# Seven q tiles in the ring of x tiles, and a new hand-over order, in a two-part long-convolution and state-space kernel

## Chip, cores and metric

One NeuronCore of a Trainium2 chip runs the whole program in one launch. The metric is the device time in microseconds; the median of eight runs of the kernel before is 384.14 us. PE is TensorE, ACT ScalarE, DVE VectorE, POOL GpSimd; SP is the engine that only issues DMAs here.

## The reference

Two branches share nothing and their results are put side by side, 1024 channels each, over 2048 time steps, in bf16.

```python
# A: a short convolution, a gate, a convolution as long as the sequence, a gate
k_shift = sum(k_pad[:, t:t + S, :] * shift_k[:, ks - 1 - t] for t in range(4))
kv = k_shift * v
y = irfft(rfft(pad(kv)) * rfft(pad(ssm_k)))[:, :S] + kv * ssm_D
a = q * y
# B: a diagonal complex recurrence between two complex matrices
Bu = einsum("bld,pd->blp", x, B_bar)
h_t = Lam_bar * h_(t-1) + Bu_t
b = 2 * einsum("blp,dp->bld", hseq, C).real + x * Dskip
out = concatenate([a, b], axis=-1)
```

## The kernel before

The program is a list of tasks. Each task is a small function that emits the instructions of one step for one tile; the string ORDER names them, and the last loop of `full_kernel` calls them one after the other. Each engine executes its own instructions in the order in which the tasks stand in ORDER, and semaphores tie the engines together. So ORDER is five queues written into one another. A task's name is followed by its indices: `y.15.1.3` is the last quarter of the second half of y for chunk 15.

**Branch B** works on 16 chunks of 128 time steps.
- `x.i` loads a chunk transposed into the ring `xT` of seven tiles (the first three by way of PE). `U.i.jp` (PE, L478, 32 matmuls) forms a quarter of B x in the PSUM pool `ps_u` (two banks); `ue.i.jp` (ACT, L480) evicts it into `u`.
- DVE runs the recurrence of a chunk: `r1.i` rotates u (L490), `r2.i` adds (L499), `ca.i` adds the carry (L504), `sc.i` scans (L510, two instructions), `cm.i` and `cy.i` make the next carry (L515, L517), `r3.i` rotates back (L490), `r4.i` adds (L523) and leaves h.
- `y.i.dh.part` (PE, L534 and L539) multiplies h by C and adds x D in `ps_y` (one bank), for the second half of the chunks 14 and 15 in `ps_u`. `ye.i.dh` (ACT, L549) evicts it, `yst.i` (POOL, L551) stores it, `ysh` (SP, L555) stores the last chunk in halves. `y.i.1.1` is the last reader of a tile of `xT`.

**Branch A** is a Fourier transform of length 4096 in two steps, with a trip to DRAM between them.
- `k`, `v` load; `kvm`, `kva`, `kvb`, `kvc` (DVE, L579 to L597) form kv; `am`/`ae`/`ast` do the first step for kv, `hT`/`hc`/`hm`/`he`/`hst` that for the filter.
- For 32 groups of frequencies: `lh`, `l`, `lw` load the group's data (tiles for two groups at a time), `sh` and `sk` (PE, L684) do the second step for filter and kv, `she` and `ske` (ACT) evict, `sw` (POOL) swaps halves by DMA, `pr` (DVE, L717) multiplies, `sa` (PE, L726) goes back, `sae` (ACT, L737) evicts, and `vst` (POOL, L739) stores two groups into the DRAM tensor `Vs`. The tile `vsb` that it stores from has two buffers.
- After the last `vst`, for 16 tiles: `vl.n` loads a tile of `Vs` (SP, L744, two DMAs, five buffers `vv`), `ql.n` loads q (SP, L749), `a3.n.w` (PE, L756) does the last step for one half, `a3e.n.w` (ACT, L764) evicts it into `ot`, `qm.n` multiplies by q (DVE, L775) and `ost.n` stores (POOL, L777). For the tiles 13, 14 and 15 `qp.n.w` (DVE, L770) multiplies straight from PSUM and `oth.n.w` (SP, L772) stores a half.

The q tiles have six buffers `qt` in a pool that opens where the pool of the `l2k` tiles (the kv spectra that `l` loads) ends, so no q tile loads before the last `sk`. The seventh waits until the `qm` of an earlier one has freed its buffer.

Of the kernel before, what the change touches and what calls it, by code (L numbers as in the profile page):

```python
# [24 lines left out]
def a_constants():  # L25
# [12 lines left out]
    for si in range(4):  # L38
# [23 lines left out]
CFG = dict(nx=3, hb=2, mt=2, u=4, xT=7, h=2, yo=2, ps_t=2, ps_u=2, ps_y=1, ps_a=3, kr=8, ld=5, acc=2, ysb=3,  # L62
           hk=3, hT=2, ysbh=2, l2=3, wts=4, swa=0, x16=3, hab=3, vsb=2, vv=5, qt=6, ot=6, bdve=8)
# [3 lines left out]
bl.0.1 bl.1.1 ld_w xl.0 k.-3 ld_par xl.1 ld_F bl.7.1 ld_G bl.0.0 k.-2 bT.0.1 bl.4.1 xl.2 bT.1.1 bc.0.1 k.-1 bl.2.1  # L67
wb.4 bc.1.1 bl.5.0 par_T wb.5 bl.4.0 p32 wb.6 bl.1.0 exp1 xt.0 bl.3.1 bl.2.0 xt.1 bl.3.0 wbe.4 dve2 k.0 x.0 bl.6.0
dve3 wb.7 x.1 x.3 wbe.5 bT.0.0 sm_pre exp2 wbe.6 hl.0.0 xt.2 wbe.7 bl.7.0 bc.0.0 tab.0 bl.5.1 wb.0 hl.0.1 wb.1 k.1 x.2
dd bT.7.1 wbe.0 bT.5.0 wbe.1 bl.6.1 tab.1 wb.2 wb.3 bc.5.0 v.0 bc.7.1 x.4 tab.2 bT.1.0 wbe.2 bT.2.1 wbe.3 bc.1.0 tab.3  # L70
k.2 x.5 bc.2.1 sin0 U.0.0 tab.4 hl.1.0 k.3 kvm.0 k.4 sin.2 bT.2.0 U.1.0 bc.2.0 ue.0.0 par_rest k.5 sin.4 bT.3.1 U.2.0
ue.1.0 kva.0 eo.0 bT.3.0 U.3.0 bc.3.1 bc.3.0 kvb.0 ue.2.0 stt.0 z1.1 bT.4.0 bT.4.1 kvm.1 ue.3.0 U.1.1 eo.1 U.3.1
ue.1.1 bc.4.1 k.6 bc.4.0 kva.1 z1.0 U.0.1 kvc.0 ue.3.1 kvb.1 eo.2 kvm.2 bT.6.0 bT.5.1 v.1 bc.6.0 am.0.0 U.2.1 ae.0.0
bc.5.1 ue.0.1 z1.2 kvm.3 bT.6.1 am.0.1 am.0.2 am.0.3 U.1.2 ae.0.2 ae.0.1 ue.2.1 stt.2 ast.0.0 ae.0.3 bT.7.0 ue.1.2
ast.0.1 bc.6.1 U.0.2 v.2 bc.7.0 stt.1 cl.0.1 cl.2.0 cl.1.0 U.0.3 kva.2 eo.3 kvc.1 ue.0.2 kvb.2 am.1.0 cl.2.1 ue.0.3
U.2.2 stt.3 kvc.2 z2 cT.2.0 r1.0 cl.3.1 cT.0.1 k.7 ae.1.0 U.3.2 cl.3.0 cc.2.0 cl.0.0 cx.5.0 ue.2.2 kva.3 cT.2.1 cc.0.1
U.2.3 cx.6.0 r2.0 ue.3.2 cc.2.1 hd.0 am.2.0 sc.0 k.8 hT.0.0 ue.2.3 cx.4.1 U.3.3 ae.2.0 hc.0.0 cx.7.1 am.2.1 am.1.1
ue.3.3 hT.0.1 ae.2.1 am.1.2 cx.7.0 cT.0.0 ae.1.1 ast.2.0 am.1.3 hc.0.1 U.1.3 ast.1.0 kvb.3 ae.1.2 cm.0 r3.0 ae.1.3
# [96 lines left out]
def full_kernel(ctx, tc, A_q, A_k, A_v, A_shift_k, A_ssm_k, A_ssm_D, B_x, B_Lre, B_Lim, B_Bre, B_Bim,  # L175
                B_Cre, B_Cim, B_log_dt, B_Dskip, out, cfg=None):
    c = dict(CFG)
    c.update(cfg or {})
    nc = tc.nc
    P = 128  # L180
    S, D = A_q.shape[-2], A_q.shape[-1]
# [73 lines left out]
    def atile(pool, tag, shape):  # L255
        return ap_pool(pool).tile(shape, BF16, name=tag, bufs=c[tag])
# [490 lines left out]
    def ql(n2):  # L747
        st["qt", n2] = atile("a3q", "qt", [P, D])
        spd(st["qt", n2][:], qr[:, n2, :])  # L749
# [90 lines left out]
```

## Time and profile before

| | us |
|---|---|
| median of eight runs | 384.14 (381.8 to 387.07) |
| the profiled execution, its own time | 382.61 |
| its span, from the first instruction to the last | 380.4 |
| PE busy | 361.1 |
| DVE busy | 329.7 |
| ACT busy | 276.8 |
| POOL busy | 124.8 |
| first load of `vv` is issued | 333.2 |
| last load of q is issued | 370.0 |

Busy shares are means over the span. The row of slices in the page shows where an engine is full; the windows give the same as microseconds for a stretch; the timeline gives the instructions one by one, with the idle time of the engine ahead of each in brackets and what ended it. A matmul is pipelined: in the timeline pairs of matmuls on 512 columns follow one another every 0.43 us, though one of them is shown with 379 ns.

### The profile page before, as it was taken

What the parts mean: (1) busy time and instruction counts of PE and PEld (TensorE: products, weight loads), DVE (VectorE), ACT (ScalarE), POOL (GpSimd) and SP (SyncE); (2) the same over time, 40 slices, a digit from 0 to 9 for tenths busy, and PEclk for the clock granted to TensorE, in tenths of its full rate; (3) what the DMA queues carried; (4) which work ended last, traced back from release to release, by engine and by line L of the source; (5) the groups of instructions that cost most, each with busy time, mean ns of one, the idle gap of its engine ahead of it and who ended that gap; (6) DMA issues with size and microseconds to landing.
All of it is one profiled execution on the core that took longest, in us unless ns stands there. A gap on an engine that the chain in (4) does not pass through costs nothing.

```text
span 380.4 us, 9007 instructions
## 1 busy us (share of the span) xinstructions
PE 361.1 (95%) x3553; PEld 246.7 (65%) x3553; DVE 329.7 (87%) x341; ACT 276.8 (73%) x511; POOL 124.8 (33%) x215
## 2 busy tenths in 40 slices
PE   5799999999999999999999999999999999699992
PEld 3499999966777777777676455545645745564440
DVE  4889999999999997999999999999972696099844
ACT  3699888778669777787427888988899988437232
POOL 3000112346365555547204323353242523102112
PEclk9999999999999999999999999999999999999997
DMA  8999599998586866455977999999999956789988
GB/s 241 338 307 269 167 223 255 271 325 263 208 265 241 217 172 202 146 183 185 308 210 230 253 307 293 360 292 282 340 273 361 315 175 191 281 278 375 408 328 298
DMA packets 60772, 101.15 MB, mean 266 GB/s; under 512 B 28445, under 2 KB 31517, under 8 KB 60730
## 3 DMA queue, kind: packets, MB, share of 16 engines
q1 hardware_dynamic: 47274, 59.51, 54.1%
q0 software_dynamic: 13376, 41.05, 31.2%
q8 instruction: 28, 0.46, 0.5%
q14 instruction: 14, 0.11, 0.1%
q10 hardware_dynamic: 80, 0.01, 0.0%
HBM read 53.10 MB, written 33.55 MB: 228 GB/s over the span
## 4 chain that ended last, share of the span: by engine, by line
PE 80%; DMA 7%; DVE 5%; ACT 4%; issue 2%; POOL 0%; DVEq 0%; ACTq 0%; POOLq 0%
PE ps_u L478 26%; PE ps_y L534 24%; PE ps_a L684 7%; PE ps_t L726 6%; PE ps_t L430 3%; PE ps_a L603 3%; PE ps_a L649 3%; PE ps_t L627 2%; PE ps_u L534 2%; DMA Ys_h<-ysbh 2%; DMA ysb<-in_B_x_dram 2%; PE ps_y L539 2%; DMA Vs<-vsb 2%; PE ps_a L756 1%; DMA kring<-in_A_k_dram 1%
## 5 line engine op out<-in xcount | busy, mean ns | idle before, releaser
L534 PE MATMUL ps_y<-CT,h 128*128 128x512 bf16 x480 | 125.1, 379 | 0.6 <-ACT yo L549 0.5
L478 PE MATMUL ps_u<-xT,BT 128*128 128x128 bf16 x2048 | 124.0, 219 | 0.0
L478 PEld LDWEIGHTS <-BT 128*128 128x128 bf16 x2048 | 119.2, 98 | 6.4
L534 PEld LDWEIGHTS <-h 128*128 128x128 bf16 x512 | 46.4, 98 | 45.9 <-DVE h L523 0.7
L510 DVE TENSOR_TENSOR_SCAN h<-rtab,h 128x1024 bf16<-128x1024 f32 x32 | 71.5, 2276 | 0.3
L664 POOL DMA_DIRECT2D Ys_h<-ysbh x64 | 46.2, 724 | 39.2 <-ACT ysbh L657 38.9
L480 ACT CAST u<-ps_u 128x512 bf16<-128x512 f32 x64 | 38.5, 602 | 25.3 <-PE ps_u L478 25.3
L737 ACT CAST vsb<-ps_t 128x512 bf16<-128x512 f32 x64 | 39.0, 642 | 9.9 <-DMA Vs<-vsb 5.7
L490 DVE TENSOR_TENSOR mt<-u,Z 128x4096 bf16<-128x4096 bf16 x16 | 36.6, 2284 | 10.3 <-ACT u L480 10.3
L657 ACT CAST ysbh<-ps_a 128x512 bf16<-128x512 f32 x64 | 35.9, 612 | 11.8 <-DMA Ys_h<-ysbh 6.3
L614 POOL DMA_DIRECT2D Ys_kv<-ysb x32 | 17.9, 561 | 77.0 <-ACT ysb L612 75.0
L612 ACT CAST ysb<-ps_a 128x512 bf16<-128x512 f32 x64 | 37.1, 605 | 6.4 <-PE ps_a L603 6.1
L706 ACT CAST x<-ps_a 128x512 bf16<-128x512 f32 x64 | 37.7, 632 | 2.6 <-PE ps_a L684 2.4
L490 DVE TENSOR_TENSOR mt<-h,Z 128x4096 bf16<-128x4096 bf16 x16 | 36.6, 2285 | 0.1
L717 DVE TENSOR_TENSOR hab<-x,hab 128x2048 bf16<-128x2048 bf16 x18 | 21.7, 1215 | 10.6 <-ACT hb L694 5.6
L579 DVE TENSOR_TENSOR mt<-kring,wbc 128x4096 bf16<-128x4096 bf16 (+3 forms) x16 | 30.1, 1883 | 0.0
L549 ACT CAST yo<-ps_y 128x512 bf16<-128x512 f32 x30 | 18.3, 609 | 15.0 <-PE ps_y L534 13.2
L539 PE MATMUL ps_y<-Dd,xT 128*128 128x128 bf16 x120 | 26.3, 219 | 0.0
L726 PEld LDWEIGHTS <-wts 128*128 128x128 bf16 x128 | 12.3, 98 | 17.8 <-issue 4.9
L603 PE MATMUL ps_a<-acc,F1t 128*128 128x512 bf16 x64 | 22.1, 379 | 0.1
L694 ACT CAST hab<-ps_a 128x512 bf16<-128x512 f32 x36 | 21.3, 621 | 0.8 <-PE ps_a L684 0.7
L539 PEld LDWEIGHTS <-xT 128*128 128x128 bf16 x128 | 12.5, 98 | 14.1 <-issue 0.9
(125 smaller groups left out, 527.2 us busy)
## 6 DMA issues: line engine op xcount, KB each, us to landing
Ys_kv<-ysb POOLq DMA_DIRECT2D x32, 256.0 KB, 3.3
Ys_h<-ysbh POOLq DMA_DIRECT2D x64, 128.0 KB, 3.1
hk<-Ys_h SPq DMA_DIRECT2D x16, 512.0 KB, 6.4
l2k<-Ys_kv SPq DMA_DIRECT2D x16, 512.0 KB, 5.9
Vs<-vsb POOLq DMA_DIRECT2D x16, 512.0 KB, 6.5
vv<-Vs SPq DMA_DIRECT2D x32, 256.0 KB, 5.4
hab<-hab POOLq DMA_DIRECT2D x36, 128.0 KB, 5.5
kring<-in_A_k_dram SPq DMA_DIRECT2D x16, 256.0 KB, 5.3
```

The costliest lines, as they stand in the source:

```text
L478: nc.tensor.matmul(pu[:, w, jl, :], BT[:, 2 * jp + jl, w, d, :], xT[:, d, :], start=(d == 0), stop=(d == ND - 1))
L480: E["ue"] = lambda i, jp: nc.scalar.copy(st["u", i][:, :, 2 * jp:2 * jp + 2, :], st.pop(("pu", i, jp))[:])
L490: nc.vector.tensor_mul(m, s_, win(Z))
L510: nc.vector.tensor_tensor_scan(gf[:, a, :], rt1, gf[:, a, :], 0.0, ALU.mult, ALU.add)
L534: nc.tensor.matmul(py[:], h[:, 1 - w, j, :], CT[:, j, w, dh * 512:(dh + 1) * 512], start=(j == 0 and w == 0), stop=(j == NJ - 1 and w == 1))
L539: nc.tensor.matmul(py[:, dl * P:(dl + 1) * P], st["xT", i][:, d, :], Dd[:, d, :], start=False, stop=False)
L612: nc.scalar.copy(st["ysb", n2, cc][:, dh * 512:(dh + 1) * 512], st.pop(("pa", n2, w))[:])
L657: nc.scalar.copy(st["yh", qd, n4, w // 2][:, :, w % 2, :], st.pop(("pa", qd, n4, w))[:].rearrange("p (c d) -> p c d", c=2))
L664: gpd(Ys_h[cc, n0:n0 + 2, :, qd * DQ:(qd + 1) * DQ].rearrange("n k d -> k n d"), t_[:, cc, :, :])
L706: nc.scalar.copy(st["x16", g][:, w * 512:(w + 1) * 512], st.pop(("ps", "l2k", g, w))[:])
L726: nc.tensor.matmul(pt[:], st["w", gq][:, gi, 1 + a, :], hab[:, a, w * 512:(w + 1) * 512], start=(a == 0), stop=(a == 1))
L737: nc.scalar.copy(st["vsb", gq][:, gi, w * 512:(w + 1) * 512], st.pop(("ps", "v", g, w))[:])
```

## The change

The tiles of q with n of 9 and more take a buffer of the ring `xT` instead of one of `qt`. The ring has seven tiles and 16 chunks of x go through it; the q tiles go on behind them, each into the buffer of an x tile that is done. The other nine q tiles stay in `qt`. ORDER is written anew: it has the same 1684 tasks, most of them within a few places of where they stood.

The code, and of ORDER the beginning and the last part:

```diff
-CFG = dict(nx=3, hb=2, mt=2, u=4, xT=7, h=2, yo=2, ps_t=2, ps_u=2, ps_y=1, ps_a=3, kr=8, ld=5, acc=2, ysb=3,
-           hk=3, hT=2, ysbh=2, l2=3, wts=4, swa=0, x16=3, hab=3, vsb=2, vv=5, qt=6, ot=6, bdve=8)
+CFG = dict(nx=3, qx=7, hb=2, mt=2, u=4, xT=7, h=2, yo=2, ps_t=2, ps_u=2, ps_y=1, ps_a=3, kr=8, ld=5, acc=2,
+           ysb=3, hk=3, hT=2, ysbh=2, l2=3, wts=4, swa=0, x16=3, hab=3, vsb=2, vv=5, qt=6, ot=6, bdve=8)
 ORDER = """
-bl.0.1 bl.1.1 ld_w xl.0 k.-3 ld_par xl.1 ld_F bl.7.1 ld_G bl.0.0 k.-2 bT.0.1 bl.4.1 xl.2 bT.1.1 bc.0.1 k.-1 bl.2.1
-wb.4 bc.1.1 bl.5.0 par_T wb.5 bl.4.0 p32 wb.6 bl.1.0 exp1 xt.0 bl.3.1 bl.2.0 xt.1 bl.3.0 wbe.4 dve2 k.0 x.0 bl.6.0
-dve3 wb.7 x.1 x.3 wbe.5 bT.0.0 sm_pre exp2 wbe.6 hl.0.0 xt.2 wbe.7 bl.7.0 bc.0.0 tab.0 bl.5.1 wb.0 hl.0.1 wb.1 k.1 x.2
-dd bT.7.1 wbe.0 bT.5.0 wbe.1 bl.6.1 tab.1 wb.2 wb.3 bc.5.0 v.0 bc.7.1 x.4 tab.2 bT.1.0 wbe.2 bT.2.1 wbe.3 bc.1.0 tab.3
...
-sa.30.1 sae.30.0 y.12.1.2 sae.30.1 sa.31.0 sa.31.1 sae.31.0 U.15.1 sae.31.1 vst.15 y.12.1.3 ue.15.1 U.14.3 ye.12.1
-yst.12 U.15.2 ue.14.3 vl.4 r1.14 vl.0 y.13.0.0 ue.15.2 vl.1 vl.7 y.13.0.1 r2.14 vl.5 U.15.3 ca.14 sc.14 y.13.0.2
-ue.15.3 y.13.0.3 a3.4.0 ye.13.0 a3.4.1 a3e.4.0 a3.0.0 vl.9 a3e.4.1 a3.0.1 a3e.0.0 y.13.1.0 qm.4 vl.3 a3e.0.1 r3.14
-ost.4 a3.1.0 a3.1.1 a3.7.0 vl.6 a3.7.1 a3e.7.0 y.13.1.1 vl.15 qm.0 a3e.7.1 a3e.1.0 cm.14 y.13.1.2 ost.0 r4.14 a3e.1.1
-a3.5.0 cy.14 a3.5.1 qm.1 a3e.5.0 y.13.1.3 r1.15 vl.2 a3e.5.1 ost.1 ql.7 a3.9.0 a3.9.1 a3e.9.0 a3.3.0 vl.11 a3e.9.1
-a3.3.1 qm.5 a3e.3.0 vl.14 a3e.3.1 r2.15 ost.5 ye.13.1 a3.6.0 yst.13 ca.15 a3.6.1 sc.15 a3e.6.0 y.14.0.0 vl.10 a3e.6.1
-ql.9 a3.15.0 a3.15.1 y.14.0.1 vl.8 y.14.0.2 y.14.0.3 qm.7 a3.2.0 r3.15 ye.14.0 ost.7 a3.2.1 y.14.1.0 vl.12 ql.15
-y.14.1.1 qm.6 a3.11.0 r4.15 ql.3 ost.6 y.14.1.2 y.14.1.3 y.15.0.0 ye.14.1 yst.14 y.15.0.1 qm.9 ost.9 y.15.0.2 y.15.0.3
-y.15.1.0 a3e.2.0 a3e.11.0 y.15.1.1 a3e.2.1 ye.15.0 qm.2 y.15.1.2 ql.14 ost.2 qp.15.0 ql.10 y.15.1.3 ql.11 qp.15.1
-ql.13 a3.14.0 qm.3 ye.15.1 a3.10.0 a3.14.1 ost.3 a3.11.1 a3.12.0 a3e.11.1 vl.13 a3e.10.0 ql.8 ql.12 oth.15.0 oth.15.1
-qm.11 ost.11 a3e.12.0 qp.14.0 qp.14.1 a3.8.0 oth.14.0 a3.10.1 oth.14.1 ysh.0 a3.12.1 ysh.1 a3e.10.1 a3e.12.1 a3.8.1
-qm.10 a3e.8.0 qm.12 ost.10 a3e.8.1 a3.13.0 ost.12 a3.13.1 qm.8 ost.8 qp.13.0 qp.13.1 oth.13.0 oth.13.1
+bl.0.1 bl.1.1 ld_w xl.0 bl.0.0 ld_par xl.1 ld_G k.-3 ld_F k.-2 xl.2 bT.0.1 k.-1 bT.1.1 bl.7.1 bc.0.1 bl.5.0 bl.4.1
+wb.4 bc.1.1 bl.1.0 par_T wb.5 wbe.4 bl.2.0 p32 wb.6 bl.2.1 exp1 xt.0 bl.4.0 bl.6.0 xt.1 k.0 x.0 bl.3.0 dve2 bl.3.1
+dve3 wb.7 wbe.6 x.1 x.3 bT.0.0 wbe.5 tab.0 exp2 xt.2 wbe.7 k.1 bc.0.0 dd bl.7.0 wb.0 v.0 wb.1 wbe.0 k.2 bT.7.1 x.4 x.2
+tab.1 wb.2 bc.7.1 wbe.1 wb.3 hl.0.1 bT.5.0 tab.2 k.3 wbe.3 bT.1.0 bl.5.1 bc.5.0 x.5 sm_pre wbe.2 bT.2.1 bc.1.0 k.4
...
+sa.30.0 vst.14 sa.30.1 sae.30.0 y.12.1.2 sae.30.1 sa.31.0 sa.31.1 sae.31.0 U.15.1 sae.31.1 vst.15 y.12.1.3 ue.15.1
+U.14.3 ye.12.1 yst.12 y.13.0.0 ue.14.3 vl.0 r1.14 y.13.0.1 vl.4 U.15.2 vl.7 vl.1 r2.14 vl.5 U.15.3 ql.15 ca.14 sc.14
+y.13.0.2 y.13.0.3 a3.0.0 a3.0.1 a3e.0.0 a3.4.0 vl.3 a3e.0.1 a3.4.1 a3e.4.0 a3.7.0 qm.0 vl.6 a3e.4.1 a3.7.1 r3.14
+a3e.7.0 ost.0 vl.9 ye.13.0 a3.1.0 ql.11 ue.15.2 ql.9 y.13.1.0 a3e.1.0 a3e.7.1 qm.4 y.13.1.1 cm.14 ost.4 r4.14 y.13.1.2
+cy.14 y.13.1.3 a3.1.1 a3.3.0 a3e.1.1 vl.2 a3.5.0 ql.10 a3.3.1 qm.1 a3e.5.0 a3.5.1 a3e.3.0 ost.1 a3.6.0 vl.15 a3e.5.1
+ye.13.1 ql.3 qm.5 vl.14 a3e.3.1 y.14.0.0 yst.13 ql.7 ue.15.3 ost.5 r1.15 y.14.0.1 y.14.0.2 y.14.0.3 r2.15 y.14.1.0
+ye.14.0 a3e.6.0 ca.15 y.14.1.1 sc.15 y.14.1.2 y.14.1.3 a3.9.0 a3.6.1 a3e.9.0 a3.2.0 vl.11 a3e.6.1 a3.9.1 a3.15.0 qm.3
+a3e.9.1 vl.10 a3.15.1 r3.15 ost.3 a3.2.1 vl.12 a3.14.0 vl.8 qm.7 r4.15 ost.7 qm.9 y.15.0.0 qm.6 ost.9 y.15.0.1 ost.6
+y.15.0.2 y.15.0.3 y.15.1.0 y.15.1.1 y.15.1.2 ql.12 a3e.2.0 qp.15.0 ql.8 ql.13 y.15.1.3 a3e.2.1 qp.15.1 oth.15.0
+ye.15.0 qp.14.0 a3.11.0 a3.10.0 qm.2 a3e.11.0 a3.14.1 a3e.10.0 ost.2 a3.11.1 qp.14.1 vl.13 a3.12.0 a3e.11.1 ysh.0
+a3.8.0 oth.15.1 a3.10.1 qm.11 oth.14.0 a3.12.1 oth.14.1 a3e.10.1 ost.11 a3e.12.0 a3.8.1 qm.10 a3e.12.1 ost.10 ye.15.1
+qm.12 a3e.8.0 ost.12 ye.14.1 a3e.8.1 yst.14 qm.8 ost.8 a3.13.0 a3.13.1 qp.13.0 qp.13.1 oth.13.0 ysh.1 oth.13.1
...
     def ql(n2):
-        st["qt", n2] = atile("a3q", "qt", [P, D])
+        st["qt", n2] = btile("xT", [P, D]) if n2 >= 16 - c["qx"] else atile("a3q", "qt", [P, D])
         spd(st["qt", n2][:], qr[:, n2, :])
```

Read off by engine, ACT's queue from `ue.14.3` to `ue.15.3` is

```text
before: ue.14.3 ue.15.2 ue.15.3
after:  ue.14.3 a3e.0.0 a3e.0.1 a3e.4.0 a3e.4.1 a3e.7.0 ye.13.0 ue.15.2 a3e.1.0 a3e.7.1 a3e.1.1 a3e.5.0
        a3e.3.0 a3e.5.1 ye.13.1 a3e.3.1 ue.15.3
```

PE's from `U.14.3` to the start of chunk 15's y (`y.14` stands for its eight tasks, where they are together) is

```text
before: U.14.3 U.15.2 y.13.0.0 y.13.0.1 U.15.3 y.13.0.2 y.13.0.3 a3.4.0 a3.4.1 a3.0.0 a3.0.1 y.13.1.0 a3.1.0
        a3.1.1 a3.7.0 a3.7.1 y.13.1.1 y.13.1.2 a3.5.0 a3.5.1 y.13.1.3 a3.9.0 a3.9.1 a3.3.0 a3.3.1 a3.6.0 a3.6.1
        y.14.0.0 a3.15.0 a3.15.1 y.14.0.1 y.14.0.2 y.14.0.3 a3.2.0 a3.2.1 y.14.1.0 y.14.1.1 a3.11.0 y.14.1.2
        y.14.1.3 y.15.0.0
after:  U.14.3 y.13.0.0 y.13.0.1 U.15.2 U.15.3 y.13.0.2 y.13.0.3 a3.0.0 a3.0.1 a3.4.0 a3.4.1 a3.7.0 a3.7.1
        a3.1.0 y.13.1.0 y.13.1.1 y.13.1.2 y.13.1.3 a3.1.1 a3.3.0 a3.5.0 a3.3.1 a3.5.1 a3.6.0 y.14 a3.9.0 a3.6.1
        a3.2.0 a3.9.1 a3.15.0 a3.15.1 a3.2.1 a3.14.0 y.15.0.0
```

and SP's from `l.15` to the end is

```text
before: l.15 ql.0 ql.5 ql.1 ql.6 ql.2 ql.4 vl.4 vl.0 vl.1 vl.7 vl.5 vl.9 vl.3 vl.6 vl.15 vl.2 ql.7 vl.11 vl.14
        vl.10 ql.9 vl.8 vl.12 ql.15 ql.3 ql.14 ql.10 ql.11 ql.13 vl.13 ql.8 ql.12 oth.15.0 oth.15.1 oth.14.0
        oth.14.1 ysh.0 ysh.1 oth.13.0 oth.13.1
after:  l.15 ql.14 ql.1 ql.5 ql.6 ql.4 ql.2 ql.0 vl.0 vl.4 vl.7 vl.1 vl.5 ql.15 vl.3 vl.6 vl.9 ql.11 ql.9 vl.2
        ql.10 vl.15 ql.3 vl.14 ql.7 vl.11 vl.10 vl.12 vl.8 ql.12 ql.8 ql.13 oth.15.0 vl.13 ysh.0 oth.15.1
        oth.14.0 oth.14.1 oth.13.0 ysh.1 oth.13.1
```

On DVE the recurrence of the last two chunks and the multiplications by q follow as r1.14 r2.14 ca.14 sc.14 qm.4 r3.14 qm.0 cm.14 r4.14 cy.14 qm.1 r1.15 qm.5 r2.15 ca.15 sc.15 qm.7 r3.15 qm.6 r4.15 before, and after as r1.14 r2.14 ca.14 sc.14 qm.0 r3.14 qm.4 cm.14 r4.14 cy.14 qm.1 qm.5 r1.15 r2.15 ca.15 sc.15 qm.3 r3.15 qm.7 r4.15.

## The prediction

> **What bounds the kernel now.** I read the page first: busy shares, then the row of slices.
>
> ```profile
> PE 361.1 (95%) x3553; PEld 246.7 (65%) x3553; DVE 329.7 (87%) x341; ACT 276.8 (73%) x511; POOL 124.8 (33%) x215
> ...
> PE   5799999999999999999999999999999999699992
> ...
> DMA  8999599998586866455977999999999956789988
> ```
>
> TensorE is full from the third slice to the end but for one dip, so between 20 and 309 us only an order that opens holes in PE can cost, and none can gain much. What can move is the opening (0 to 20 us), the dip at 323 us and the tail. Next the windows of the tail; after the stretch come PE, PEld, DVE, ACT and POOL busy, then the clock, the DMA share and GB/s.
>
> ```profile
> 345.00:350.00 5.00, 4.81 (x23) 2.04 (x21) 5.00 (x6) 3.70 (x8) 1.22 (x3) 1.00 1.03 394
> 355.00:360.00 5.00, 5.00 (x27) 2.31 (x26) 5.00 (x6) 0.59 (x2) 1.08 (x2) 1.00 1.05 408
> 365.00:370.00 5.00, 4.47 (x22) 1.95 (x21) 0.31 (x1) 1.51 (x3) 0.54 (x1) 1.00 0.73 272
> ```
>
> Until 360 us PE, DVE and the DMA engines are all full; after 365 us DVE and DMA have gaps. So which of the three ends last must come from the timeline. DVE's rows first, the last instructions of the recurrence for the chunks 14 and 15:
>
> ```profile
> 332.63 2.29 DVE L490 TENSOR_TENSOR mt<-u,Z 128x4096 bf16<-128x4096 bf16 x1 [9.56 <-ACT u L480]
> ...
> 344.56 1.23 DVE L523 TENSOR_TENSOR h<-mt 128x2048 bf16<-128x2048 bf16 x1
> ...
> 346.39 2.28 DVE L490 TENSOR_TENSOR mt<-u,Z 128x4096 bf16<-128x4096 bf16 x1
> ...
> 358.50 1.22 DVE L523 TENSOR_TENSOR h<-mt 128x2048 bf16<-128x2048 bf16 x1
> ```
>
> These are r1.14, r4.14, r1.15 and r4.15. DVE has no idle time from 332.63 to 359.7, and r4.15 ends at 359.71. What waits for it (PE's weight loads), and when ACT had evicted the last of u for chunk 15:
>
> ```profile
> 359.76 0.10 PEld L534 LDWEIGHTS <-h 128*128 128x128 bf16 x1 [0.30 <-DVE h L523]
> ```
>
> ```profile
> 337.54 0.59 ACT L480 CAST u<-ps_u 128x512 bf16<-128x512 f32 x1 [3.15 <-PE ps_u L478]
> 339.27 0.59 ACT L549 CAST yo<-ps_y 128x512 bf16<-128x512 f32 x1 [1.14 <-PE ps_y L534]
> ```
>
> So **the last scan sets the end**: y.15 starts 0.08 us after r4.15. From there the path is y.15 (to 367.15), eleven a3 halves (to 373.5), qm and qp on DVE (to 376.57), and the last store (to 380.4). ue.15.3, which r1.15 needs, was done at 338.12, over 8 us before r1.15 started. This slack is the number to watch. The q loads appear on this path once:
>
> ```profile
> ACT vsb L737 <- DMA Vs<-vsb: 5.7, 2, 4.1
> ...
> DVE ot L775 <- DMA qt<-in_A_q_dram: 1.5, 1, 1.5
> ```
>
> **What the Trainium skill says.** "PSUM — Partial Sum Buffer", section Engine vs sequencer instructions: the queues of ScalarE, VectorE and GpSimdE are strict FIFO, and matmuls start in program order. The trace agrees: each engine's rows stand in the order of ORDER. So an eviction listed late runs late, even if its PSUM was ready long before. "DMA: Bandwidth & Descriptors", section Issuing engines are not separate DMA queues: transfers from all queues interleave on the same 16 engines. The trace agrees: the store of Vs issued at 313.25 landed after 3.1 us, the one at 319.90, with six q loads beside it, after 5.8 us.
>
> **The change, part by part.**
>
> Buffers. q 9 to 15 take ring slots; the waits become y of the x tile that had the slot. For ql.14, 15, 11 and 9 these are y.9 to y.12, all past by then; for ql.10 it is y.13, for ql.13 y.14, for ql.12 y.15.1.1. No instruction is added or removed. But of the seven only ql.14 is listed ahead of the first vl; the others stand behind it on SP. So 0.25 MB leaves the tail, at some 400 GB/s 0.65 us of DMA time. Bounds: 0 to -0.65 us. It goes to about 301 us, where lh.15, l.15 and a Vs store share the engines and ACT waits 1.64 us for that store: 0 to +0.65 us. I take zero for the two. The six loads for qt slots stay beside the Vs store of 319.90, so the dip at 323 us (3.4 us) stays.
>
> Opening. xl.2 and bl.0.0 stand earlier on SP. PE waited 2.11 us for xl.2's tile at 13.27. But bT.2.0 now comes before U.0.0, U.0.0 needs the fifteenth load in both orders, and sin.4 (1.1 us of ACT) comes before bc.2.0 and ue.0.0, so U.2.0 and U.3.0 wait for ACT. I put it at -0.3, bounds -1.5 and +0.8.
>
> Middle. Adding the row durations along each queue, the work on PE ahead of y.i.0.0 and that on DVE ahead of r4.i agree within 0.1 us in both orders for i = 5 to 8, where the slack is smallest (0.06, 0.66, 1.28, 2.59 us). k.6 to k.10, v.14 and x.10 move back by 60 to 100 places, all still ahead of their use. x.10 now waits for y.4, and U.10.0 comes some 70 places later. A few PSUM slots get tighter (an hm at 137, an sa at 237 us). Taken: +0.3, bounds -0.3 and +2.0.
>
> Tail up to y.15. PE does the same work until 339.06 (U.15.2, U.15.3 and y.13.0 in another sequence), and U.14.3 with ue.14.3 stays, so r1.14 is at 332.6 and r4.14 at 345.8 as before. But **ue.15.3 moves**: in ACT's queue twelve a3e, ye.13.0, ue.15.2 and ye.13.1 now stand between ue.14.3 and it; before, only ue.15.2 did. Replayed with this trace's pitches (an a3 half 0.43 us on PE, y.13.1 3.88, an eviction 0.49 from start to start, 0.59 long):
> - a3.0.0 at 339.06; a3e.0.0 at 339.7, the fifth (7.0) at 341.65, ye.13.0 from 342.1 to 342.7.
> - y.13.1 needs ye.13.0's bank: 342.8 to 346.7. Then a3.1.1, 3.0, 5.0, 3.1, 5.1: the last ends at 349.0.
> - ACT: a3e.5.1 from 349.15, ye.13.1 from 349.65, a3e.3.1 from 350.1, ue.15.3 from 350.6 to 351.2.
> - DVE: qm.1 and qm.5 are done at 350.4; r1.15 starts at 351.25 instead of 346.39, that is 4.9 us late, and DVE stands idle for some 4 us.
> - From r1.15's start to r4.15's end it took 13.3 us with three qm in between; now there are two: 12.7. r4.15 ends at 363.95, **4.2 us late**.
>
> PE meanwhile has y.14 (350.25 to 358.0) and eight a3 halves (to 361.5), then nothing: it idles 2.5 us for r4.15. The lower bound of the delay: without the hold of y.13.1 it is 0.7 us less, so 3.5; the upper, with a vv tile landing late, 5.
>
> Tail after y.15. y.15 runs 364.05 to 371.4. Eleven a3 halves follow, as before. vl.13 waits for a3.14.1 (372.8); before, a3.13 began 3.9 us after vl.13's issue, so now at 376.8, in time. On ACT ye.15.1 and ye.14.1 now stand ahead of a3e.8.1, which ends at 378.1; then qm.8 and two qp (0.6 each): 380.0; the last store lands 3.8 us after its issue, as at 376.6 before: 383.9. q 12 and 8 load when y.15.1.1 is done (368.3) and land well before their qm, so the 1.5 us wait goes; a3e.8.1 is late in its stead. From y.15's end it is 12.5 us, against 13.25 before: a gain of 0.7.
>
> **Sum**, against the profiled run: scan +4.2, end -0.7, opening -0.3, middle +0.3, buffers 0: +3.5. The span goes from 380.4 to 383.9 us. That run took 382.61, 2.2 around its span, and stands 1.5 under the median of 384.14. On the median: 387.6.
>
> **The rivals.**
> - *The transfers decide* (faster). DMA share is 1.03 to 1.05 from 340 to 365 us; if the end hung on that stream, seven tiles of 0.65 us would be worth up to 4.5 us, and the one wait for q, 1.5 us, is real. Against it: PE has no wait for vv worth naming up to 366 us, six of the seven loads are still listed behind vl, and SP now blocks at vl.11 until a3.6.1. It decides only if r1.15 can start before some 347 us. It would give some 2.5 us less: 381.6.
> - *The opening pays back* (no change). Most of the 2.11 us wait for xl.2 is won, U starts 1.5 to 2 us earlier, and everything behind it, since DVE's waits up to 151 us are for PE; with the late scan: 385.8.
> - *The middle breaks* (slower still). The tight PSUM slots each cost most of a microsecond on PE and the loads at 301 us delay the Vs store: 389.6.
> - *It does not do what it says*: with one q tile ahead of vl it is an order change with a new label. This is part of my forecast.
>
> **How the numbers follow.** The late scan, with the middle and the opening within their bounds but no large payback: 0.68, of that a little in "same". The payback: 0.14. The transfers: 0.10. The middle: 0.08. A measurement of this kernel tells some 0.5% (1.9 us) from no change; so faster 0.11, same 0.19, slower 0.70. The likeliest is 387.6. The range reaches down into the payback case (383.0) and up to the broken middle (390.3).
>
> **What would show it.** Right: L480's last eviction at about 350 us, right behind an L549 and an L764; DVE idle before the last L490 on u, put down to ACT u L480, for about 4 us; PE or PEld waiting 2 us for DVE h L523 ahead of the last y; DMA share under 1 between 353 and 359 us; no wait for qt. Wrong: r1.15 within 1 us of 346.4 after alignment at r1.14, or r1.14 itself shifted by over 1.5 us, which would put the difference into the opening, or the dip at 323.

## The result, and the profile after

The kernel after takes 389.67 us (median of 11 runs, 387.72 to 392.87); the kernel before, beside it, 384.39 us (32 runs, 381.8 to 388.61). The ratio is **1.0137, with a 95% interval of 1.0106 to 1.0168**: 5.3 us slower. The profiled execution took 389.05 us with a span of 387.3, against 382.61 and 380.4 before.

The page of the kernel after, busy shares and the rows of slices:

```profile
PE 365.1 (94%) x3553; PEld 249.3 (64%) x3553; DVE 330.1 (85%) x341; ACT 277.0 (72%) x511; POOL 124.9 (32%) x215
...
PE   5899999999999999999999999999999988999692
...
PEclk9999999999999999999999999999999989999997
```

The dip of before, one 6 at 323 us, has become two 8s from 310 to 329 us, and there is a new 6 in the slice from 358 us. PE is "busy" 4 us longer with the same 3553 matmuls. Some 1.7 us of that are in the row PEclk, an 8 in the slice from 310 us: for 3.4 us TensorE ran at half its clock. The windows around it and in the tail, again of the kernel after (columns as before: PE, PEld, DVE, ACT, POOL busy, clock, DMA share, GB/s):

```profile
314.00:316.00 2.00, 1.40 (x4) 0.46 (x4) 2.00 (x3) 2.00 (x5) 1.37 (x3) 0.71 0.37 90
316.00:318.00 2.00, 2.00 (x6) 0.73 (x5) 1.58 (x3) 1.33 (x3) 1.28 (x3) 0.50 0.81 295
...
345.00:350.00 5.00, 4.42 (x25) 2.02 (x23) 3.87 (x5) 2.27 (x5) 1.02 (x2) 1.00 1.03 350
350.00:355.00 5.00, 4.15 (x23) 1.94 (x22) 2.30 (x3) 3.62 (x7) 1.61 (x3) 1.00 1.05 401
355.00:360.00 5.00, 5.00 (x28) 2.38 (x26) 4.83 (x4) 1.07 (x2) 0.00 (x0) 1.00 1.04 402
360.00:365.00 5.00, 4.09 (x19) 1.67 (x17) 5.00 (x4) 2.74 (x5) 0.54 (x1) 1.00 0.66 194
365.00:370.00 5.00, 2.94 (x17) 1.51 (x18) 4.99 (x8) 0.00 (x0) 1.64 (x3) 1.00 0.90 311
```

Before, DVE was full from 345 to 350 us; now it stands idle for a fourth of that window and for half of the next, and it is full from 365 to 370 us, where it was nearly idle before. The timeline of DVE in the kernel after says why (r4.14, qm.1, qm.5, r1.15, r4.15):

```profile
347.59 1.22 DVE L523 TENSOR_TENSOR h<-mt 128x2048 bf16<-128x2048 bf16 x1
...
350.78 0.69 DVE L775 TENSOR_TENSOR ot<-ot,qt 128x1024 bf16<-128x1024 bf16 x1 [1.88 <-ACT ot L764]
352.62 0.69 DVE L775 TENSOR_TENSOR ot<-ot,qt 128x1024 bf16<-128x1024 bf16 x1 [1.15 <-ACT ot L764]
354.09 2.29 DVE L490 TENSOR_TENSOR mt<-u,Z 128x4096 bf16<-128x4096 bf16 x1 [0.78 <-ACT u L480]
...
365.79 1.22 DVE L523 TENSOR_TENSOR h<-mt 128x2048 bf16<-128x2048 bf16 x1
```

Three brackets with 3.8 us of idle time stand between the two chunks, where before there was none. All three name ACT. ACT's own timeline in the kernel after: the last two rows ahead of ue.15.3 (an L480) are ye.13.1 and a3e.3.1.

```profile
352.46 0.62 ACT L549 CAST yo<-ps_y 128x512 bf16<-128x512 f32 x1
352.94 0.63 ACT L764 CAST ot<-ps_t 128x512 bf16<-128x512 f32 x1
353.41 0.64 ACT L480 CAST u<-ps_u 128x512 bf16<-128x512 f32 x1
```

And what PE's weight loads waited for at chunk 15's y, in the same trace:

```profile
367.05 0.10 PEld L534 LDWEIGHTS <-h 128*128 128x128 bf16 x1 [3.46 <-DVE h L523]
```

The bracket that held 0.30 us before holds 3.46. The same, summed over the run, among the waits of the kernel after:

```profile
ACT vsb L737 <- DMA Vs<-vsb: 6.5, 3, 3.2
...
PEld L534 <- DVE h L523: 3.5, 1, 3.5
```

ACT's wait for the store of Vs, 5.7 us before, is now 6.5. No wait of DVE for q is left among the 40 longest; before, one cost 1.5 us.

From these rows and the tasks' starts (us from the start of the span):

| | before | after | later by |
|---|---|---|---|
| U.13.0 starts | 267.88 | 268.19 | 0.3 |
| r1.13 starts | 298.94 | 300.30 | 1.4 |
| store vst.11 issued, landed | 302.14, 309.33 | 303.50, 311.75 | 1.4, 2.4 |
| r1.14 starts | 332.63 | 335.66 | 3.0 |
| ue.15.3 ends | 338.12 | 354.06 | 15.9 |
| r1.15 starts | 346.39 | 354.09 | 7.7 |
| r4.15 ends | 359.71 | 367.00 | 7.3 |
| y.15 ends | 367.31 | 374.59 | 7.3 |
| span | 380.4 | 387.3 | 6.9 |

So this pair of executions lost 3.0 us ahead of r1.14, 4.3 us from there to r4.15, and won back 0.4 us behind y.15. It is 6.9 us apart where the medians are 5.3 apart: the profiled execution of before had no stretch at half clock while PE had work and lies 1.8 us below its median, that of after had one.

### The profile page after: what moved, and what is told of

It is laid out like the page before. It is cut to its first block, busy times and chain, and to the rows that moved or that the text cites. A ratio compares the mean times of both kernels' runs of the same rounds, so it can differ in the third digit from the quotient of the medians.

```text
span 387.3 us, 9012 instructions
## 1 busy us (share of the span) xinstructions
PE 365.1 (94%) x3553; PEld 249.3 (64%) x3553; DVE 330.1 (85%) x341; ACT 277.0 (72%) x511; POOL 124.9 (32%) x215
## 5 line engine op out<-in xcount | busy, mean ns | idle before, releaser
L478 PE MATMUL ps_u<-xT,BT 128*128 128x128 bf16 x2048 | 125.6, 221 | 0.0
L478 PEld LDWEIGHTS <-BT 128*128 128x128 bf16 x2048 | 120.7, 99 | 7.0
L480 ACT CAST u<-ps_u 128x512 bf16<-128x512 f32 x64 | 38.4, 601 | 18.5 <-PE ps_u L478 18.4
L717 DVE TENSOR_TENSOR hab<-x,hab 128x2048 bf16<-128x2048 bf16 x18 | 21.8, 1215 | 15.1 <-ACT x L706 6.8
```

The costliest lines, as they stand in the source:

```text
L478: nc.tensor.matmul(pu[:, w, jl, :], BT[:, 2 * jp + jl, w, d, :], xT[:, d, :], start=(d == 0), stop=(d == ND - 1))
L480: E["ue"] = lambda i, jp: nc.scalar.copy(st["u", i][:, :, 2 * jp:2 * jp + 2, :], st.pop(("pu", i, jp))[:])
```

## The experiments

Edits of ORDER are shown as the tasks around the place. Ratios are to the kernel before, with a 95% interval. "Old order" and "new order" are those of the kernels before and after.

### The late scan

**e1_scan_early**, the kernel after with the last two evictions of u ahead of the a3 evictions, and r1.15 ahead of the two qm:

```diff
-y.13.0.2 y.13.0.3 a3.0.0 a3.0.1 a3e.0.0 ... ye.13.0 a3.1.0 ql.11 ue.15.2 ...
-a3.3.1 qm.1 ... qm.5 vl.14 a3e.3.1 y.14.0.0 yst.13 ql.7 ue.15.3 ost.5 r1.15 y.14.0.1
+y.13.0.2 y.13.0.3 a3.0.0 a3.0.1 ue.15.2 ue.15.3 a3e.0.0 ... ye.13.0 a3.1.0 ql.11 ...
+a3.3.1 r1.15 qm.1 ... qm.5 vl.14 a3e.3.1 y.14.0.0 yst.13 ql.7 ost.5 y.14.0.1
```

> The changed kernel with ue.15.2 and ue.15.3 placed ahead of the first a3e on ACT and r1.15 ahead of qm.1 and qm.5 on DVE; nothing else moves. Theory of the late scan: r1.15 starts 0.6 us after r4.14 instead of 5.3, r4.15 comes 4.2 us earlier, and the span falls from 387.3 by about 4 us to 383.3 (ratio to the kernel before about 1.003 to 1.005). Rival, the transfers: SP stays blocked at vl.11 until a3.6.1, so the tail ends with the stream and the span falls by 1 us or less.

Measured: 386.08 us, ratio 1.0042 [1.0018, 1.0067], so 0.94% or 3.6 us off the kernel after. In its trace r1.15 starts the moment r4.14 is done. Not all of the scan's loss is gone, though. DVE's timeline in this kernel, from r1.15 on (r1.15, qm.5, qm.3, r4.15):

```profile
350.27 2.28 DVE L490 TENSOR_TENSOR mt<-u,Z 128x4096 bf16<-128x4096 bf16 x1
...
354.07 0.69 DVE L775 TENSOR_TENSOR ot<-ot,qt 128x1024 bf16<-128x1024 bf16 x1 [0.91 <-ACT ot L764]
...
361.13 0.69 DVE L775 TENSOR_TENSOR ot<-ot,qt 128x1024 bf16<-128x1024 bf16 x1 [0.46 <-DMA qt<-in_A_q_dram]
...
364.54 1.22 DVE L523 TENSOR_TENSOR h<-mt 128x2048 bf16<-128x2048 bf16 x1
```

qm.1 and qm.5 have moved into the recurrence of chunk 15, and with them their wait for ACT, and qm.3 now waits for q. From r1.15's start to r4.15's end it takes 15.5 us, against 13.3 before and 12.9 after. From r1.14's start to r4.15's end: 27.1 us before, 31.3 after, 28.6 here. My edit removes 2.7 of the 4.3 us.

**e1_evict_only**, one execution, the same with r1.15 left behind qm.1 and qm.5:

```diff
-a3.0.1 a3e.0.0 ... ue.15.2 ... ue.15.3 ost.5 r1.15
+a3.0.1 ue.15.2 ue.15.3 a3e.0.0 ... ost.5 r1.15
```

> The same with the two evictions moved alone; r1.15 stays behind qm.5 on DVE. If the late scan has two locks, ACT's order and DVE's, r1.15 now waits for qm.5, which waits for a3e.5.1: r1.15 starts some 0.5 to 1 us earlier than in the changed kernel relative to r1.14 (18.4 us there) and the span falls by under 1 us. If ACT's order was the only lock, it falls by 4 us.

ue.15.3 is done at 341.43, and r1.15 still starts 17.6 us behind r1.14 (18.4 after, 13.8 before): only 0.9 us are won. DVE's timeline in this kernel (qm.1, qm.5, r1.15):

```profile
351.06 0.69 DVE L775 TENSOR_TENSOR ot<-ot,qt 128x1024 bf16<-128x1024 bf16 x1 [1.87 <-ACT ot L764]
352.90 0.69 DVE L775 TENSOR_TENSOR ot<-ot,qt 128x1024 bf16<-128x1024 bf16 x1 [1.15 <-DMA vv<-Vs]
353.51 2.28 DVE L490 TENSOR_TENSOR mt<-u,Z 128x4096 bf16<-128x4096 bf16 x1
```

The second bracket names a DMA, but a3e.5.1 ended at 352.87, 0.03 us ahead of that row, so it is ACT here too. The scan had **two locks on it**: its input came late by ACT's queue, and qm.1 and qm.5, themselves late by a3e.1.1 and a3e.5.1, stood ahead of it in DVE's queue. The second alone holds it, as this run shows. The first alone was not run; that it would hold it too follows from the kernel after, where ue.15.3 itself ends at 354.06. By the trace PE's order adds to both: a3.1.1 now stands behind the whole of y.13.1, so in the kernel after it starts at 349.74, and ACT is idle for 2.9 us ahead of a3e.1.1, with ue.15.3 further back in its queue. No run moved y.13.1.

**s2_old_then_new**: the first 1399 tasks (up to l.15, some 303 us) in the old order, the remaining 285 in the new one, with the ring.

```diff
-ORDER = new
+ORDER = the first 1399 of old, then the others as they stand in new
```

> The first 1399 tasks in the order of the kernel before (up to about 302 us), the rest in the order of the changed kernel, buffers as changed. If the loss arises after 302 us, the span is 380.4 plus 2.6 (ql.14 and the clock) minus 0.9 plus 4.3 minus 0.4, that is 386 (ratio about 1.013). If the order ahead of 302 us brings the tail into its bad state, it is under 384.

388.24 us (5 runs), ratio 1.0083 [1.005, 1.0117]: less than the 1.013 forecast for a loss that all arises behind 302 us, so a part of it lies ahead. r1.15 starts 18.4 us behind r1.14, as in the kernel after, and r4.15 ends 31.3 us behind it, also as there. From r1.13 to r1.14 it takes 33.5 us, against 33.7 before, so in this one trace the new order from 303 to 333 us costs nothing that shows. What the new tail costs is 0.83%, some 3.2 us.

### The loads of q and the buffers

**b2_ring_only**, the ring for q 9 to 15 in the old order (the diff is against the kernel after, whose line for the ring stays):

```diff
         st["qt", n2] = btile("xT", [P, D]) if n2 >= 16 - c["qx"] else atile("a3q", "qt", [P, D])
-ORDER = new
+ORDER = old
```

> The changed buffers with the order of the kernel before. If the ring by itself does nothing to the path, the span stays within 1 us of 380.4: q loads on SP no longer wait for qm, but r4.15 at 359.7 still sets the end; the 1.5 us wait of qm.12 for its load may go, and ql.13 waits for y.15.1.1. If the transfers of the tail set the end, the span falls by 2 us or more.

384.83 us, 1.0017 [0.9992, 1.0043]. The buffers by themselves do nothing that can be told; the 1.5 us wait of DVE for q, in qm.12, is still there.

**b1_ql14_early**, the kernel before with q 14 alone in the ring, loaded behind l.15:

```diff
-pr.24 l.15 ske.26.1 ... y.15.1.2 ql.14 ost.2
+pr.24 l.15 ql.14 ske.26.1 ... y.15.1.2 ost.2
```

> The kernel before with one q tile, q 14, in the ring and its load moved behind l.15; all else as before. Theory of the collision: the landing of vst.11 comes 0.6 to 1.0 us later, PE's hole at 310 to 313 us grows, and if the clock follows the hole it drops to about 0.5 for 2 us: the span grows by 1 us without and by 2.5 us with the drop. Rival: one q tile less in the tail pays it back: no difference.

384.51 us, 1.0018 [0.999, 1.0045]. The store vst.11 lands 8.1 us after its issue, against 7.2 before; the time does not show it, and the growth by 1 us or more that was forecast did not come.

**e2_ql14_late**, the reverse, the kernel after with ql.14 behind vl.5:

```diff
-l.15 ue.15.0 ql.14 she.28.1 ... r2.14 vl.5 U.15.3
+l.15 ue.15.0 she.28.1 ... r2.14 vl.5 ql.14 U.15.3
```

> The changed kernel with ql.14 moved on SP from behind l.15 to behind vl.5, ahead of ql.15. Theory: ql.14 shares the DMA engines with the Vs store vst.11 and delays its landing by 1.0 us (11.75 minus 9.33, less the 1.35 by which it is issued later); ACT's wait before sae.26.0 falls from 2.67 to about 1.65 us, and PE's granted clock stays at 1.00 between 314 and 318 us, where the changed kernel shows 0.71 and 0.50; together 2.6 us off the arrival at vst.13, span about 384.7 to 385.5. Rival: the drop of the clock has another cause (PE's own order there): 1 us only, 386.3, with the clock low as before.

388.98 us (4 runs), 1.0115 [1.0078, 1.0152], against 1.0137 for the kernel after; the intervals overlap widely. vst.11 still lands after 8.8 us without ql.14 beside it, and the half clock has only moved to 329.5 us. So ql.14 alone is not what delays that store or lowers the clock; **this expectation fell**.

**b3_q_behind_vl**, the kernel before with its first six loads of q behind the first vl, to see whether the loads of q in the dip are worth anything:

```diff
-ql.0 ske.31.1 sa.29.1 ql.5 ql.1 y.12.1.1 sae.29.0 ql.6 sae.29.1 ql.2 pr.31 ql.4 sa.30.0 vst.14
+ske.31.1 sa.29.1 y.12.1.1 sae.29.0 sae.29.1 pr.31 sa.30.0 vst.14
...
-vl.4 r1.14 vl.0 y.13.0.0 ue.15.2 vl.1 vl.7 y.13.0.1 r2.14 vl.5 U.15.3
+vl.4 r1.14 vl.0 ql.4 y.13.0.0 ue.15.2 vl.1 ql.0 vl.7 ql.1 y.13.0.1 r2.14 vl.5 ql.5 ql.6 ql.2 U.15.3
```

> The kernel before with its six first q loads moved on SP behind the first loads of vv (ql.4 behind vl.0, ql.0 behind vl.1, ql.1 behind vl.7, ql.5, 6 and 2 behind vl.5). Theory: the store vst.13 then has the DMA engines nearly alone and lands in about 3.1 us instead of 5.8; the dip at 323 us shrinks by up to 2.7 us and all behind it moves up: span 377.7 to 378.5, ratio 0.993 to 0.995. Rival: the six tiles lengthen the full stream of the tail by 3.9 us and come late for qm.4 and qm.0, which stand in front of r3.14 and cm.14 on DVE: no gain or a loss of up to 2 us.

385.9 us, 1.0061 [1.0035, 1.0088], where a gain (0.993 to 0.995) had been forecast. The dip closes: vst.13 lands after 3.2 us instead of 5.8, the hole in PE shrinks from 3.2 to 0.6 us, r1.14 starts at 328.92, 3.7 us early. All of it is given back and more: PE waits 3.5 us for tiles of `vv`, r4.15 ends only 1.6 us early (DVE waits for q inside the recurrence), y.15 starts 1.5 us late. DVE's timeline in this kernel, the wait in the recurrence of chunk 15:

```profile
353.44 0.69 DVE L775 TENSOR_TENSOR ot<-ot,qt 128x1024 bf16<-128x1024 bf16 x1 [1.97 <-DMA qt<-in_A_q_dram]
```

**b4_q_on_pool** gives those six loads to POOL, behind vst.14:

```diff
-ql.0 ske.31.1 sa.29.1 ql.5 ql.1 y.12.1.1 sae.29.0 ql.6 sae.29.1 ql.2 pr.31 ql.4 sa.30.0 vst.14
+ske.31.1 sa.29.1 y.12.1.1 sae.29.0 sae.29.1 pr.31 sa.30.0 vst.14 ql.0 ql.5 ql.1 ql.6 ql.2 ql.4
...
-        spd(st["qt", n2][:], qr[:, n2, :])
+        (gpd if n2 in (0, 1, 2, 4, 5, 6) else spd)(st["qt", n2][:], qr[:, n2, :])
```

> The kernel before with its six first q loads issued by POOL behind vst.14 instead of by SP: they then start some 2.8 us later, behind the stores vst.13 and vst.14 and ahead of vst.15, and not in the stream of the tail as in b3. vst.13 should land in 3.2 us (as in b3) and the dip at 323 us shrink from 3.4 to below 1 us, so r1.14 comes 2.5 to 3.5 us earlier; the tail has the same loads as before and keeps its length. Span 377.5, ratio 0.991 to 0.994. Rival: vst.15 now stands behind the six loads and lands late by as much, so vl starts at 333 as before and a3 holds the tail: ratio 1.00.

385.44 us, 1.0028 [1.0006, 1.005]; the gain that was forecast (0.991 to 0.994) did not come here either. The dip closes here too, but the six loads now stand beside the last store: vst.15 lands after 7.8 us (4.6 before), and the first vl, which needs it, comes late. My reading of b3 and b4: the bytes have to pass somewhere between 320 us and the end; moved, they delay something else. This agrees with what the Trainium skill says of DMAs from different engines ("DMA: Bandwidth & Descriptors", section Issuing engines are not separate DMA queues): they run on the same 16 engines and interleave.

### The steps ahead of 303 us

**s1_new_then_old**, the mirror of s2: the first 1399 tasks new, the rest old.

```diff
-ORDER = new
+ORDER = the first 1399 of new, then the others as they stand in old
```

> The first 1399 tasks in the order of the changed kernel, the rest in the order of the kernel before, buffers as changed. PE is 1.4 us late at 302 us in the changed kernel. If that passes through to the end, the span is 381.8 and the ratio about 1.004. If the dip behind 309 us absorbs it, it is 380.4; if the arrival of the first part is what upsets the stretch from 309 to 324 us, it is 383 to 384.

386.48 us, 1.005 [1.0026, 1.0074]. So the new order costs 0.5% ahead of 303 us, and with the 0.83% of s2 that makes 1.33%, where the whole is 1.37%. Where, shows first at one swap. The timelines of DVE at pr.19 (an L717), in the kernel before and after:

```profile
281.09 1.23 DVE L717 TENSOR_TENSOR hab<-x,hab 128x2048 bf16<-128x2048 bf16 x1 [0.23 <-ACT x L706]
```

```profile
283.39 1.22 DVE L717 TENSOR_TENSOR hab<-x,hab 128x2048 bf16<-128x2048 bf16 x1 [2.14 <-DMA hab<-hab]
```

pr.19 now waits for its swap, sw.19. In the old order the load lh.13 is issued at 279.14, 1.8 us behind the swap's second half; in the new one at 278.23, 0.04 us behind it. The second half lands 5.1 us after its issue instead of 3.2.

**s3_lh13_later**, s1 with that load put back behind l.12:

```diff
-she.21.0 lh.13 sk.19.0 sw.20 ... cy.12 l.12 sk.20.0
+she.21.0 sk.19.0 sw.20 ... cy.12 l.12 lh.13 sk.20.0
```

> As s1 (first 1399 tasks in the new order, the rest in the old one), with the load lh.13 moved on SP from ahead of lw.12 to behind l.12. Theory: in all five runs with the new order lh.13 (0.5 MB) is issued 0.5 us behind the swap sw.19 instead of 2.3 us, the swap's second half lands after 5.2 to 7.2 us instead of 2.9 to 4.6, pr.19 and sa.19 are late and PE has a hole of 1 to 2 us between 282 and 291 us. Now sw.19 lands within 4.6 us, U.13.0 to r1.13 takes 31.2 us instead of 32.1 to 33.4, and the ratio falls from 1.005 to about 1.001. Rival: the hole comes from the order of ACT in that stretch and stays: 1.005.

385.29 us, 1.0032 [1.0006, 1.0057]. pr.19's wait in this kernel, from DVE's timeline:

```profile
281.35 1.23 DVE L717 TENSOR_TENSOR hab<-x,hab 128x2048 bf16<-128x2048 bf16 x1 [0.92 <-DMA hab<-hab]
```

In s1 it was 2.35 us, and pr.19 started at 283.28. From U.13.0 to r1.13 it is 31.5 us here, and 33.3 in s1. The trace shows the collision go; the times (1.005 to 1.0032, where 1.001 was forecast) move the right way by less than their intervals, so by the times it is not shown.

**m1_new_middle_only**: the first 1140 tasks old, the next 259 new, the rest old. The new stretch begins just ahead of U.12.3 (some 257 us) and ends, like that of s1, at l.15; where the expectation has y.13.0 for its end, it is wrong.

```diff
-ORDER = new
+ORDER = the first 1140 of old, then as new up to 1399 tasks, then as old
```

> Ring for q 9 to 15; the first 1140 tasks in the old order, the next 259 (from U.12.3 to just ahead of y.13.0) in the new one, the rest in the old one. Theory: what the new order loses ahead of the tail is lost between U.13.0 and r1.13 and at the store of Vs behind it (the traces so far: 32.1 to 33.4 us from U.13.0 to r1.13 with the new order, 30.9 to 31.8 with the old): ratio 1.004 to 1.006, as for the new order up to y.13 (1.005), and 32 us or more from U.13.0 to r1.13. Rival: it is lost earlier, in the opening or in the steps up to U.12: ratio 0.999 to 1.002, and 31 to 31.8 us from U.13.0 to r1.13.

385.99 us (22 runs), 1.0036 [1.0014, 1.0057]. The number lies between the two forecasts, nearer to the first, and its interval shares only a corner with the second. In the trace sw.19's second half lands after 6.4 us and pr.19 waits 3.02 us for it; that is an indication only, since the profiled execution is one of the longest of this kernel (388.28 us). So most of the 0.5% is probably lost between 257 and 303 us; what is left for the time ahead of it, 0.14%, is too small to tell.

**e4_three_undone**, the kernel after with three edits at once: those of e1, ql.14 behind vl.5, lh.13 behind l.12.

```diff
-a3.0.1 a3e.0.0 ... ue.15.2 ... qm.1 ... qm.5 ... ue.15.3 ost.5 r1.15
+a3.0.1 ue.15.2 ue.15.3 a3e.0.0 ... r1.15 qm.1 ... qm.5 ... ost.5
-l.15 ue.15.0 ql.14 she.28.1 ... vl.5 U.15.3
+l.15 ue.15.0 she.28.1 ... vl.5 ql.14 U.15.3
-she.21.0 lh.13 sk.19.0 ... l.12 sk.20.0
+she.21.0 sk.19.0 ... l.12 lh.13 sk.20.0
```

> The changed kernel with all three causes undone and the rest of its order kept: the evictions and r1.15 early (as e1), ql.14 late (as e2), lh.13 behind l.12. If the three make up the loss, the ratio to the kernel before is 0.998 to 1.003, against 1.0137 for the change. If something else of the new order costs as much as lh.13, it is 1.004 or more.

386.75 us, 1.0054 [1.003, 1.0078]: no better than e1 alone, and outside the forecast for three causes that make up the loss (0.998 to 1.003). The trace says why for a good part. From r1.14's start to r4.15's end it takes 29.5 us, still 2.4 more than before, by the waits that my own edit put into the recurrence; DVE's timeline in this kernel (qm.5 and qm.3):

```profile
352.46 0.69 DVE L775 TENSOR_TENSOR ot<-ot,qt 128x1024 bf16<-128x1024 bf16 x1 [0.91 <-ACT ot L764]
...
360.33 0.69 DVE L775 TENSOR_TENSOR ot<-ot,qt 128x1024 bf16<-128x1024 bf16 x1 [1.27 <-DMA qt<-in_A_q_dram]
```

The rest is not settled. No version that I ran is faster than the kernel before.

## Why the prediction was right, and where it was off

387.6 us was predicted and 389.67 measured. The late scan and the end came about as predicted; the 2.1 us between the two numbers are for the most part the middle, which was put too low.

**The late scan: right, in mechanism and size.** Against r1.14 of its own run the replay said: ue.15.3 done 18.6 us behind it (measured 18.4), r1.15 4.9 us late (measured 4.7), r4.15 4.2 us late (measured 4.3), PE idle 2.5 us ahead of y.15 (the weight loads' bracket grew by 3.2). The two locks were both in the replay, since qm.1 and qm.5 were counted ahead of r1.15, though it named only ACT's; e1_evict_only shows that the second alone still costs 3.8 of the 4.7 us. The statement of the Trainium skill that it used ("PSUM — Partial Sum Buffer", section Engine vs sequencer instructions, strict FIFO queues on ScalarE and VectorE) is borne out: PE had finished U.15.3 at 340.53, and its eviction began at 353.41.

**The end: right in sign.** From y.15's end to the span's end 12.7 us instead of 13.1 in the profiles, a gain of 0.4 where 0.7 was predicted. q is no longer waited for. Scan and end together were put at +3.5; s2 measures 0.83% or 3.2 us [1.9, 4.5].

**The buffers: right in sum.** Zero taken; b2 and b1 measure 0.17% and 0.18% with intervals that reach to zero. Two of the waits were misread, without effect. ql.12 was put behind y.15.1.1, but in the kernel after it is issued at 365.31, ahead of y.15's start at 367.06. ql.13 was put behind y.14; it is issued at 367.63, right when a qm ends (367.61), so it takes the buffer of a q tile that is done and not that of an x tile.

**The opening: not to be told from zero.** y.5.0.0 starts at 170.4 on average over the seven profiles with the old order up to there, and at 170.0 over the seven with the new one, with a scatter of 2 to 3 us in each.

**The middle: mis-sized.** In "Taken: +0.3, bounds -0.3 and +2.0" the value was too small, though within its bounds. s1 measures 0.5% or 1.9 us [1.0, 2.8] for all that comes ahead of 303 us, and m1 0.36% or 1.4 us [0.5, 2.2] for the part from U.12.3 on. My working compared the sums of row durations on PE and DVE at y.i and r4.i; that shows how much work stands ahead of a step, but not what a load does to a transfer in flight beside it. And it stopped at i = 8, while the loss lies at i = 12 and 13. With lh.13 right behind sw.19 (kernel after, e1_scan_early, e1_evict_only, e2, s1, m1) U.13.0 to r1.13 takes 32.1 to 33.4 us, 32.8 on average; with the same new order and lh.13 later (s3, e4) 31.5 and 31.7; with the old order 30.9 to 31.8, 31.2 on average. The 1.9 us of s1 are close to the whole gap between 387.6 predicted and 389.67 measured. The traces put some 1.2 us of them down to the one load. The times do not show it: s3 lies below s1 by less than the intervals, and e4, which has lh.13 late as well, is no faster than e1.

**Two signs were wrong.** "DMA share under 1 between 353 and 359 us": it was 1.04 from 355 to 360, and the dip (0.66) came at 360 to 365. And I said r1.14 would stay at 332.6; it came 3.0 us later, over the 1.5 us that I had named as a mark against me. 1.4 us of that stood already at r1.13; the rest is about what the half clock costs, 1.7 us, which was not in the working at all.

**The rivals.** *The transfers decide* is out for this change: the kernel is slower, the ring alone wins nothing (b2), and in the kernel after y.15 starts 0.06 us behind r4.15. They are a close second, though. In b3 and b4, with the dip freed, y.15 starts 3.2 and 1.2 us behind r4.15, so there the scan alone no longer sets the end. *The opening pays back* did not show. *The middle breaks* was nearer than its chance of 0.08 says: its 389.6 is what was measured, and the steps ahead of 303 us cost 0.5% of the 1.37%. By the traces that comes in the main from the swap beside lh.13, and not from ql.14 alone (e2); the PSUM slots that this rival named were not tested. *It does not do what it says* holds for the buffers: without the new order they are worth nothing (b2).

**Open.** In the kernels after, e1_scan_early, e2, s3, e4 and m1 the store vst.11 lands 8.3 to 9.3 us after its issue, against 6.3 to 7.2 in before, b2, b3, b4 and s2; s1 has 6.8, e1_evict_only 7.8 and b1 8.1. Neither ql.14 nor lh.13 alone accounts for it, and I did not find what does. Nor is it shown what s3 still loses (1.0032), and e4 beyond the 2.4 us in the recurrence.

## What to carry to other kernels

When an order is written anew, follow each in-order queue to the last producer of the critical step, and list what now stands ahead of it on both the producer's and the consumer's queue; replayed with the pitches of the trace, that gave the delay to 0.2 us here. Freeing one of two such queues won 0.9 of 4.7 us. Do the same for transfers that an engine waits for: a sum of work per engine sees nothing of a load that is issued 0.04 us instead of 1.8 us behind a swap.

## What the runs showed of the hardware

**The half clock.** In the profiles of the kernel after and of nine of the twelve experiments the granted clock falls to 0.5 once while PE still has work, for 3.4 us each time, between 313 and 353 us; in those of before, s2, b4 and e1_evict_only it falls only behind the last matmul. It takes 1.7 us of matmul time, so two single profiles of this kernel can differ by that much. The traces show when it comes. All changes of the clock in a trace lie whole multiples of 3.41 us apart, so each trace can be cut into periods of that length, counted from its first change (at 19 to 25 us). The matmul work in a period is my estimate: each matmul counts from its start for the pitch of its kind, 0.216 us on 512 columns, 0.109 on 256 and 0.056 on 128. Of the 1444 periods at full clock in the 14 traces, the 24 with work in up to 0.345 of their time are each followed by half clock, and of the 1420 with 0.380 or more none is.

So it matters how a hole lies among the periods. The hole of 3.23 us in PE at 323 us in the kernel before falls across two of them, which keep 0.55 and 0.49, and nothing follows; a hole of 3.24 us in b2_ring_only, with the same order, falls within one (0.14), and half clock follows. In the kernel after four holes of 1.14, 0.27, 0.27 and 0.76 us between 311 and 314.9 us (from one matmul's start to the next, less its usual 0.22 us) leave 0.32 in one period. "TensorE: Matmul & The Clock Gate", section Part 1: The HAM clock gate, in the Trainium skill says that the clock halves after an idle window of about 3.4 us. The length agrees, but here a window with matmuls in up to a third of it was enough. No run was made to test this apart.

The half clock explains little of the result: among executions with a mean clock of 0.993 or 0.994, the kernel after takes 388.4 us (3 runs) and the kernel before 383.6 (53 runs); at 0.988 to 0.990, 389.8 (3 runs) and 384.6 (85 runs).

**A store alone and beside loads.** The 0.5 MB of vst.13 land after 5.8 us with six loads of q beside them and after 3.2 us without (b3); the second half of sw.19, 128 KB, lands after 3.2 us with the load lh.13 issued 1.8 us behind it (before) and after 5.1 us with it issued 0.04 us behind (after). Over the 14 traces it is 3.0 to 4.6 us with that load 1.8 us or more behind and 5.1 to 7.2 us with it 0.04 us behind.
